# One visit per slot for the V products of an attention kernel: moved batch softmaxes, a fourth bank for the score maxima, and V products in one of the scores' PSUM banks

## The chip, the core and the metric

The kernel runs on one core of a Trainium2 chip. The metric is the device time of one execution in microseconds (us). Before the change the median of three runs is 297.95 us (297.89 to 298.03). The profile is one further execution; its span, from the first to the last instruction, is 299.0 us. Engines are named as in the profile: PE (TensorE, matmuls), PEld (its weight loads), DVE (VectorE), ACT (ScalarE), POOL (GpSimd), SP (SyncE).

## What is computed

An attention over 8 batches, 12 heads, 448 tokens and a head size of 64, followed by a soft mixture of experts with 32 slots (8 experts of 4 slots). Cut to what matters:

```python
scores = matmul(q, k.transpose(0, 1, 3, 2)) / sqrt(64)
m = max(scores, axis=-1)
e = exp(scores - m)
x = (e / (sum(e) + exp(-m) + 1e-9)) @ v        # -> x: 3584 tokens x 768
logits = x @ phi                                # 3584 x 32
d = softmax(logits, axis=0); slot_in = d.T @ x  # over all tokens
slot_out[e] = relu(slot_in[e] @ w1[e]) @ w2[e]  # 768 -> 1024 -> 768
out = softmax(logits, axis=1) @ slot_out
```

## The kernel before

Heads are taken in pairs: 48 pairs, six to a batch. The order of the work on every engine is written out by hand. A short list of words (`ramp`, lines 716 to 757) orders the first pairs; a loop over **slots** `s` (lines 758 to 832), one per pair from 3 on, orders the rest; then follow the last softmax and the expert layers (from line 843). The loop is what the change rewrites.

What a slot holds, with the functions' names:

- **A** (L285 and L304 on PE, L287 and L307 on DVE): the maxima. PE computes the scores of a later pair once into a bank of pool `psA`, and DVE reduces that bank to one maximum per row. Seven such tiles belong to a pair: two heads for each of three blocks of 128 tokens, and one tile for the last 64 tokens of both heads.
- **Bk** (L367, L370, L396, L399 on PE, L372 and L402 on ACT): PE computes the same scores transposed into a bank of pool `psB`, a second matmul (the bias, with `sel` and `mT`) subtracts the maximum, and ACT takes the exponential out of the bank. A pair has four blocks `i`; i = 0, 1, 2 fill two banks each and i = 3 fills one: seven exponentials. In the loop the matmuls of A and Bk alternate between the two halves of the PE rows, so two run side by side.
- **T** (L256 on PE): 28 small transposes of q and k for a pair six slots ahead, into one `psB` bank; a copy empties it, on ACT (L263) where n % 6 is 1 or 3, on DVE (L265) otherwise.
- **AV** (L436 on PE): the products of the exponentials with V, 32 matmuls per pair, into the one bank of pool `psV`. **N1** (L449, ACT) copies that bank to `ubuf`; **N2** (L464, L465 on DVE; L469, L479, L480 on POOL) divides.
- **PX** (L501 on PE, L507 on ACT): the turn of x, four matmuls into one `psB` bank and a copy, for the pair two slots back.
- **W1** (POOL), **W2** (L336, L337 on PE), **W3** (L342, L345, L348 on ACT): once per three pairs the maxima are turned into the bias `mT`, and into `ec`, the exponentials of the negative maxima.
- **P(b)**: the softmaxes and the slot sums of a finished batch, six parts at places `at_z`: `l_mm` (L535, 24 matmuls), `l_ev` (L558, ACT) and `c_max`; `l_turn`; `s_max`; `exps` and `corr` (L596, L601 on ACT); `c_turn`; `s_mm` (L623, 28 matmuls) with `s_add` (L632, DVE).

The order of one slot before, two half visits: blocks 0 and 1, then the second half of the V products of pair s-1 and N1; then blocks 2 and 3, T, W2 and W3, the first half of the V products of pair s, PX. PSUM has eight banks: three in `psA`, four in `psB`, one in `psV`. A pool hands out the bank that was given back first in the program's order. A slot uses nine or ten `psB` banks in turn (2, 2, 2, 1 for the blocks, T, PX, and the bias where there is one), so a matmul that needs a bank waits for ACT or DVE to empty the tile about four places back.

```python
psA = pool("psA", 3, space=PSUM)
psB = pool("psB", 4, space=PSUM)
psV = pool("psV", 1, space=PSUM)
```

The work of a slot repeats every six slots, since T's copy goes by n % 6, W2 and W3 by s % 3 and P(b) by the batch. "Slot type" below is s modulo 6. Before, types 1 and 3 have T's copy on ACT; types 2 and 5 have the bias; `l_mm` falls in type 2, `exps` in type 4 and `s_mm` in type 0.

Of the kernel before, what the change touches and what calls it, by code (L numbers as in the profile page):

```python
# [31 lines left out]
def kernel(  # L32
# [21 lines left out]
    NPAIR = B * PB  # L54
# [102 lines left out]
    with ExitStack() as at:  # L157
# [4 lines left out]
        psB = pool("psB", 4, space=PSUM)  # L162
        psV = pool("psV", 1, space=PSUM)
        pb_ = lambda nm: psB.tile([128, 512], F32, tag="b", name=nm)
        nat = {}
        ubuf = pu.tile([128, 2, 7 * W65], F32, name="ubuf")

# [73 lines left out]
        def T(n):  # L241
            g, pl = divmod(n, NP)
            first = n < NP * NP
            ps = psB.tile([128, 2, S], BF16, tag="b", name="ps_t")

            k0 = [psB.tile([128, 2, S], BF16, tag="b", name="ps_k") for _ in range(2)] if n == 0 else None
            for a in range(2):
                src = nat["qk"[a], g]
                order = [(tok, hl) for tok in range(7) for hl in range(2)]
                if a and n == 0:  # L250
                    order.sort(key=lambda z: kcol(z[1], z[0]))
                for tok, hl in order:
                    c = kcol(hl, tok) if a else (2 * tok if tok < 4 else 2 * tok - 7) * 64
                    r = slice(64 * hl, 64 * hl + 64)
                    o = k0[c // 256][r, 0, c:c + 64] if a and n == 0 else ps[r, a, c:c + 64]
                    nc.tensor.transpose(o, src[r, pl, tok * D:(tok + 1) * D], ident[r, r])  # L256
            t = qk_t[n % NQK]
            if n == 0:
                nc.scalar.copy(t[:, 0, :], ps[:, 0, :])
                nc.vector.tensor_copy(t[:, 1, 0:256], k0[0][:, 0, 0:256])  # L260
                nc.vector.tensor_copy(t[:, 1, 256:S], k0[1][:, 0, 256:S])
            elif first or n % 6 in (1, 3):
                nc.scalar.copy(t, ps)  # L263
            else:
                nc.vector.tensor_copy(t, ps)  # L265
            qkT[n] = t
# [7 lines left out]
        def A(n, i, steps=False):  # L274
            g, pl = group[n]
            if g not in mx:
                mx[g] = psm.tile([128, 21], F32, tag="mx", name="mx")
            t = qkT[n]
            if steps:
                m = mx[g]  # L280

                def run(hl):
                    r = slice(64 * hl, 64 * hl + 64)
                    ps = psA.tile([128, 512], F32, tag="a", name="ps_a")
                    nc.tensor.matmul(ps[:, 0:S], t[r, 0, i * 128:(i + 1) * 128], t[r, 1, :], start=True, stop=True)  # L285
                    c = HG * i + 2 * pl + hl
                    nc.vector.reduce_max(m[:, c:c + 1], ps[:, 0:S], axis=AX.X)  # L287

                return [lambda: run(0), lambda: run(1)]
            if i < 3:  # L290
                pss = [psA.tile([128, 512], F32, tag="a", name="ps_a") for _ in range(2)]
                for hl in range(2):
                    r = slice(64 * hl, 64 * hl + 64)
                    nc.tensor.matmul(pss[hl][:, 0:S], t[r, 0, i * 128:(i + 1) * 128], t[r, 1, :],  # L294
                                     start=True, stop=True)
                for hl in range(2):
                    c = HG * i + 2 * pl + hl
                    nc.vector.reduce_max(mx[g][:, c:c + 1], pss[hl][:, 0:S], axis=AX.X)  # L298
            else:
                ps = psA.tile([128, 512], F32, tag="a", name="ps_a")  # L300

                for hl in range(2):
                    r = slice(64 * hl, 64 * hl + 64)
                    nc.tensor.matmul(ps[64 - 64 * hl:128 - 64 * hl, 0:S], t[r, 0, 384:448], t[r, 1, :],  # L304
                                     start=True, stop=True)
                c = 3 * HG + pl
                nc.vector.reduce_max(mx[g][:, c:c + 1], ps[:, 0:S], axis=AX.X)  # L307
# [32 lines left out]
        def W3(g):  # L340
            t = psm.tile([128, S], BF16, tag="mT", name="mT")
            nc.scalar.copy(t, st["ps_m"][:, 0:S])  # L342
            mT[g] = t
            e = psm.tile([128, NP, 7], F32, tag="ec", name="ec", bufs=3)
            nc.scalar.activation(e[:, :, 0:6].rearrange("p l (i h) -> p i l h", i=3),  # L345
                                 ngm[g][:, 0:18].rearrange("p (i l h) -> p i l h", i=3, h=2),
                                 AF.Exp, scale=scale)
            nc.scalar.activation(e[:, :, 6], ngm[g][:, 18:21], AF.Exp, scale=scale)  # L348
            ec[g] = e
# [65 lines left out]
        def av_tile(n):  # L415

            if n >= NPAIR - 3:
                return psA.tile([128, 512], F32, tag="a", name="ps_av")
            return psV.tile([128, 512], F32, tag="v", name="ps_av")

        def AV(n, i, qs):
            g, pl = divmod(n, NP)
# [93 lines left out]
        def P(b):  # L516
# [1 line left out]
            eng = nc.gpsimd if b < B - 2 else nc.vector  # L518
            x = xb[b % 2]
            v = {}  # L520
            pa = lambda shape, dt, nm: psA.tile(shape, dt, tag="a", name=nm)
            flat = lambda t: t.rearrange("p i s -> p (i s)")

            def l_mm(js):
# [138 lines left out]
        post = {}  # L663
        for b in range(B - 1):
            for z, f in enumerate(P(b)):
                at_z = (0, 1, 2, 4, 5, 9) if late(b) else (0, 1, 2, 3, 4, 6)
                post.setdefault(2 * (PB * b + PB + 2) + at_z[z], []).append(f)

        ub = ubuf.rearrange("p n c -> p (n c)").bitcast(BF16)
# [32 lines left out]
        def slot_loads(s):  # L702
# [6 lines left out]
            if s % 3 == 0 and g - 2 < NG - 1:  # L709
# [3 lines left out]

        ramp = ("T0 A A T1 A A W0 T2 A G0 A X0 J0 A B0.0 A B0.1 A A T3 A B0.2 A A T4 C0.3 V0.0 W1 A V0.1 V0.2 A X1 T5 "
                "A B1.0 A K0 V0.3 H0 C1.1 N0 B1.2 A T6 C1.3 V1.0 V1.1 A B2.0 M0 K1 A T7 B2.1 A V1.2 V1.3 W2 T8 H1 A "
                "N1 B2.2 Y2 V2.0 X2 C2.3 Z0 V2.1 M1 K2 ")
        for word in ramp.split():
            op, arg = word[0], [int(z) for z in word[1:].split(".") if z]  # L720
            if op == "T":
# [7 lines left out]
            elif op == "X":  # L729
                W2(*arg)  # L730
                W3(*arg)
            elif op == "V":
                AV(*arg, range(3))
            elif op == "H":
# [20 lines left out]
                PX(0)  # L755
            elif op == "K":
                slot_loads(*arg)
        for s in range(3, NPAIR + 1):
            for y in range(2):
                hs = 2 * s + y  # L760
                mix = len(runs) > 1 and runs[0][1] == 1 - y
# [12 lines left out]
                else:  # L774
                    As(1)
                if y == 0:
                    for i in (2, 3):
                        AV(s - 1, i, range(3))
                else:
                    if s < NPAIR - 6:  # L780
                        T(s + 6)
                    if s and s + 1 in firsts:
                        W2(mg(s + 1))
                        W3(mg(s + 1))
                    if s < NPAIR:
                        for i in (0, 1):
                            AV(s, i, range(3))
# [2 lines left out]
                if y and 0 <= s - 2 < NPAIR - 2:  # L790
                    PX(s - 2)
                if y == 0:
                    if 0 <= s - 1:
                        for i in range(4):
                            AV(s - 1, i, [3])
                        if s == NPAIR:
                            PX(s - 2)
                        N1(s - 1)
                        if not on_pool(s - 1):
                            N2(s - 1)  # L800
                else:
                    if 0 <= s - 1 and on_pool(s - 1):
                        N2(s - 1)
                if y == 0 and s and s + 1 in firsts:
                    W1(mg(s + 1))
                if y == 0 and wait_loads:
                    f, z = wait_loads.pop()
                    f(z)
                if y == 0 and s % 3 == 2 and (s + 1) // 3 < NG:
                    if s == NPAIR - 4:  # L810
                        V(NG - 1)
                    if s - 1 in half_at:
                        load_half(half_at[s - 1], 0, w_tile(half_at[s - 1]))
                if y == 0 and s - 1 in stage_at:
                    stage_rows(*stage_at[s - 1][0])
                if y == 0 and s - 2 in half_at:
                    load_half(half_at[s - 2], 1)
                if y == 0 and s - 2 in stage_at:
                    stage_rows(*stage_at[s - 2][1])
                if y == 0 and hs in rows_at:  # L820
                    load_rows(rows, rows_at[hs])
                    rows = rows_at[hs]
            if s > 2 and s + 2 in firsts:
                wait_loads.append((slot_loads, s))
            else:
                slot_loads(s)
            if 2 * s + 1 in rows_at:

                if 2 * s + 1 == 89:
                    load_rows(7, 9)  # L830
                load_rows(rows + 2 * (rows == 7), rows_at[2 * s + 1])
                rows = rows_at[2 * s + 1]
        load_rows(rows, 35)
        nc.gpsimd.memset(spread, 0.0)
        for i in range(4):
            r = slice(NS * i, NS * i + NS)
# [195 lines left out]
```

## Time and profile before

| what | value |
| --- | --- |
| median of three runs | 297.95 us |
| the profiled execution: span, first to last instruction | 299.0 us |
| PE, DVE, ACT, POOL busy | 271.4, 249.7, 249.8, 195.9 us |
| granted clock of PE, slots' loop | 1.00 |
| six stretches of six slots each, from first exponential to first exponential (slots 3 to 38) | 28.18, 28.92, 29.62, 30.78, 29.49, 29.64 us |
| T's copy: ACT (L263), DVE (L265), mean of one | 928, 615 ns |

The only time on record for the profiled execution is its span. Busy time counts an instruction from its start to its end; instructions of one engine overlap there by some tens to hundreds of ns, so the start-to-start distance of instructions that follow each other is the better price of one. The six stretches run from 33.95 us to 210.58 us, from the first exponential of a slot s with s % 6 = 3 to the next such; they cover slots 3 to 38.

### The profile page before, as it was taken

What the parts mean: (1) busy time and instruction counts of PE and PEld (TensorE: products, weight loads), DVE (VectorE), ACT (ScalarE), POOL (GpSimd) and SP (SyncE); (2) the same over time, 40 slices, a digit from 0 to 9 for tenths busy, and PEclk for the clock granted to TensorE, in tenths of its full rate; (3) what the DMA queues carried; (4) which work ended last, traced back from release to release, by engine and by line L of the source; (5) the groups of instructions that cost most, each with busy time, mean ns of one, the idle gap of its engine ahead of it and who ended that gap; (6) DMA issues with size and microseconds to landing.
All of it is one profiled execution on the core that took longest, in us unless ns stands there. A gap on an engine that the chain in (4) does not pass through costs nothing.

```text
span 299.0 us, 12398 instructions
## 1 busy us (share of the span) xinstructions
PE 271.4 (91%) x5174; PEld 162.5 (54%) x5174; DVE 249.7 (84%) x581; ACT 249.8 (84%) x559; POOL 195.9 (66%) x391
## 2 busy tenths in 40 slices
PE   5999899999999999999899999999999999996820
PEld 4445456566666566566556666656665555652100
DVE  5899799999999989999889999998999675537930
ACT  3569999999899989998989899989999987337820
POOL 8792887979696979887879697978686633000000
PEclk9999999999999999999999999999999999997555
DMA  7999998999999999999999999999799989908997
GB/s 132 147 143 208 149 138 138 188 165 188 185 204 179 184 176 202 163 182 182 202 159 184 176 199 152 196 183 196 125 150 187 213 185 263 344 10 318 380 453 322
DMA packets 47015, 58.67 MB, mean 196 GB/s; under 512 B 2800, under 2 KB 39920, under 8 KB 46704
## 3 DMA queue, kind: packets, MB, share of 16 engines
q0 software_dynamic: 40304, 42.29, 89.6%
q1 hardware_dynamic: 6656, 15.60, 13.8%
q8 instruction: 40, 0.66, 0.8%
q14 instruction: 15, 0.12, 0.1%
HBM read 89.16 MB, written 15.14 MB: 349 GB/s over the span
## 4 chain that ended last, share of the span: by engine, by line
PE 68%; ACT 10%; DVE 6%; POOL 6%; issue 4%; DMA 2%; DVEq 0%; POOLq 0%; ACTq 0%
PE ps_av L436 15%; PE ps_a L285 10%; PE ps_b L367 7%; PE ps_b L370 7%; PE ps_t L256 5%; PE ps_b L396 5%; PE ps_x L501 3%; PE ps_b L399 3%; ACT W L402 2%; PE ps_o L925 2%; DVE mx L298 2%; PE ps_s L623 2%; PE ps_h L862 2%; PE ps_so L882 2%; ACT W L263 2%
## 5 line engine op out<-in xcount | busy, mean ns | idle before, releaser
L287 DVE TENSOR_REDUCE mx<-ps_a 128x1 f32<-128x448 f32 x250 | 137.3, 613 | 4.6 <-PE ps_a L285 3.5
L372 ACT ACTIVATE W<-ps_b 128x448 bf16<-128x448 f32 x250 | 120.4, 574 | 0.0
L285 PE MATMUL ps_a<-W 64*128 64x448 bf16 x250 | 80.9, 352 | 0.0
L367 PE MATMUL ps_b<-W 64*128 64x448 bf16 x250 | 70.5, 352 | 1.1
L436 PE MATMUL ps_av<-W 128*128 128x65 bf16 (+1 forms) x1536 | 64.9, 196 | 2.2 <-issue 1.6
L436 PEld LDWEIGHTS <-W 128*128 128x128 bf16 (+1 forms) x1536 | 50.5, 100 | 30.2 <-issue 26.4
L370 PE MATMUL ps_b<-mT,sel 64*128 64x448 bf16 x250 | 66.5, 350 | 0.0
L469 POOL TENSOR_TENSOR W<-ubuf,rec 128x384 bf16<-128x384 f32 x44 | 36.3, 824 | 35.7 <-ACT W L507 19.3
L402 ACT ACTIVATE W<-ps_b 128x448 bf16<-128x448 f32 x86 | 46.1, 574 | 2.0 <-PE ps_b L399 2.0
L256 PEld LDWEIGHTS <-W 64*64 64x64 bf16 x1344 | 29.3, 112 | 12.7 <-issue 4.3
L507 ACT CAST W<-ps_x 128x512 bf16<-128x512 f32 x47 | 28.6, 608 | 7.4 <-PE ps_x L501 7.2
L256 PE MATMUL ps_t<-ident,W 64*64 64x64 bf16 x1330 | 30.6, 195 | 2.4 <-ACT W L215 1.4
L307 DVE TENSOR_REDUCE mx<-ps_a 128x1 f32<-128x448 f32 x48 | 29.5, 615 | 1.4 <-PE ps_a L304 1.4
L285 PEld LDWEIGHTS <-W 64*128 64x128 bf16 x250 | 23.4, 94 | 9.8
L114 POOL DMA_DIRECT2D W<-in_moe_w_dram x30 | 22.6, 755 | 7.9 <-PE ps_b L399 7.8
L370 PEld LDWEIGHTS <-sel 64*128 64x128 bf16 x250 | 19.6, 94 | 14.4 <-issue 5.6
L396 PE MATMUL ps_b<-W 64*64 64x448 bf16 (+1 forms) x134 | 27.1, 374 | 0.3
L449 ACT COPY ubuf<-ps_av 128x455 f32<-128x455 f32 x44 | 25.1, 571 | 0.8 <-POOL W L408 0.6
L399 PE MATMUL ps_b<-mT,sel 64*64 64x448 bf16 (+1 forms) x134 | 25.1, 354 | 0.1
L263 ACT COPY W<-ps_t 128x896 bf16<-128x896 bf16 x21 | 19.5, 927 | 6.5 <-PE ps_t L256 6.5
L298 DVE TENSOR_REDUCE mx<-ps_a 128x1 f32<-128x448 f32 x38 | 21.1, 616 | 1.9 <-PE ps_a L294 1.9
L480 POOL TENSOR_TENSOR W<-ubuf,rec 128x128 bf16<-128x128 f32 x44 | 17.5, 398 | 3.7
(156 smaller groups left out, 446.6 us busy)
## 6 DMA issues: line engine op xcount, KB each, us to landing
W<-in_moe_w_dram POOLq DMA_DIRECT2D x24, 768.0 KB, 9.9
W<-in_v_dram POOLq DMA_DIRECT2D x32, 192.0 KB, 6.5
out_dram<-W SPq DMA_DIRECT2D x2, 2688.0 KB, 10.0
W<-in_q_dram POOLq DMA_DIRECT2D x15, 336.0 KB, 6.3
W<-in_k_dram POOLq DMA_DIRECT2D x15, 336.0 KB, 7.5
stage<-in_moe_w_dram POOLq DMA_DIRECT2D x4, 768.0 KB, 9.6
W<-stage SPq DMA_DIRECT2D x4, 576.0 KB, 7.3
out_dram<-W SPq DMA_DIRECT2D x6, 384.0 KB, 3.0
```

Source lines behind the costliest of these rows:

```text
L256: nc.tensor.transpose(o, src[r, pl, tok * D:(tok + 1) * D], ident[r, r])
L285: nc.tensor.matmul(ps[:, 0:S], t[r, 0, i * 128:(i + 1) * 128], t[r, 1, :], start=True, stop=True)
L287: nc.vector.reduce_max(m[:, c:c + 1], ps[:, 0:S], axis=AX.X)
L307: nc.vector.reduce_max(mx[g][:, c:c + 1], ps[:, 0:S], axis=AX.X)
L367: nc.tensor.matmul(pss[hl][:, 0:S], t[rs[hl], 1, cols], t[rs[hl], 0, :], start=True, stop=False)
L370: nc.tensor.matmul(pss[hl][:, 0:S], sel[rs[hl], 2 * pl + hl:2 * pl + hl + 1].to_broadcast([64, 128]), mT[mg(n)][rs[hl], :], start=False, s ...
L372: nc.scalar.activation(e[:, hl, :], pss[hl][:, 0:S], AF.Exp, scale=scale)
L396: nc.tensor.matmul(outs[hl], t[rs[hl], 1, cols], t[rs[hl], 0, :], start=True, stop=False)
L399: nc.tensor.matmul(outs[hl], sel[rs[hl], 2 * pl + hl:2 * pl + hl + 1].to_broadcast([64, m]), mT[mg(n)][rs[hl], :], start=False, stop=True)
L402: nc.scalar.activation(e, p[:, 0:S], AF.Exp, scale=scale)
L436: nc.tensor.matmul(o, eT[n, i, hl][:, qc], vp[g % 2][:, 2 * pl + hl, i, 0:W65], start=(i == 0 and u == 0 and hl == 0) or (u == 3 and i == ...
L469: eng.tensor_mul(x[:, 0:3, c:c + 128].rearrange("p i (h d) -> p i h d", h=2), u[:, 0:6, 0:D].rearrange("p (i h) d -> p i h d", h=2), rec[: ...
```

## The change

The steady loop now runs over slots 3 to 44 in a new order, and the old loop is kept for the last slots alone. Per slot: blocks 0, 1, 2, 3; T; N2 of the pair before; parts of P(b); then all V products of pair s with PX between them; W2 and W3's copy of `mT`; the products of the last 64 rows; N1; and W4, the two exponentials that were the second part of W3. `pa_` takes the single `psV` bank into the turn of the `psA` banks, four in all, and the V products take a `psB` bank instead. T's copy moves from DVE to ACT for n % 6 = 4. The parts of P(b) move: `exps` from slot type 4 to 5; the others keep their slot, but `l_mm` and `s_mm` stand between T and the V products. The ramp is reordered to match: it now ends with all of pair 2's V products.

```diff
+        turn_at = {"a": 0, "whole": True}
+        def pa_(shape, dt, nm):
+            z = turn_at["a"] = (turn_at["a"] + 1) % 4
+            if z == 0 and turn_at["whole"]:
+                return psV.tile(shape, dt, tag="v", name=nm)
+            if not turn_at["whole"]:
+                turn_at["a"] = 0
+            return psA.tile(shape, dt, tag="a", name=nm)
...
-            elif first or n % 6 in (1, 3):
+            elif first or n % 6 in (1, 3, 4):
                 nc.scalar.copy(t, ps)
...
-                    ps = psA.tile([128, 512], F32, tag="a", name="ps_a")
+                    ps = pa_([128, 512], F32, "ps_a")
...
             mT[g] = t
+
+        def W4(g):
             e = psm.tile([128, NP, 7], F32, tag="ec", name="ec", bufs=3)
...
-            return psV.tile([128, 512], F32, tag="v", name="ps_av")
+            return pb_("ps_av")
...
-                at_z = (0, 1, 2, 4, 5, 9) if late(b) else (0, 1, 2, 3, 4, 6)
+                at_z = (1, 3, 5, 6, 7, 9) if late(b) else (0, 1, 2, 3, 4, 6)
...
-        ramp = ("T0 A A T1 A A W0 T2 A G0 A X0 J0 A B0.0 A B0.1 A A T3 A B0.2 A A T4 C0.3 V0.0 W1 A V0.1 V0.2 A X1 T5 "
-                "A B1.0 A K0 V0.3 H0 C1.1 N0 B1.2 A T6 C1.3 V1.0 V1.1 A B2.0 M0 K1 A T7 B2.1 A V1.2 V1.3 W2 T8 H1 A "
-                "N1 B2.2 Y2 V2.0 X2 C2.3 Z0 V2.1 M1 K2 ")
+        ramp = ("T0 A A T1 A A W0 T2 A G0 A X0 J0 A B0.0 A B0.1 A A T3 A B0.2 A A T4 C0.3 V0.0 W1 A V0.1 V0.2 A X1 V0.3 H0 "
+                "N0 T5 A B1.0 A K0 C1.1 B1.2 A T6 C1.3 V1.0 V1.1 A M0 V1.2 V1.3 H1 N1 B2.0 K1 A T7 B2.1 A A W2 T8 B2.2 "
+                "Y2 X2 C2.3 Z0 V2.0 V2.1 M1 V2.2 V2.3 H2 N2 K2 ")
...
+        SN = NPAIR - 3
...
+        for s in range(3, SN):
+            Bk(s, 0, mix=True)
+            Bk(s, 1, mix=True)
+            if s + 1 in firsts:
+                W1(mg(s + 1))
+            half_loads(s, 0)
+            for f in post.get(2 * s, ()):
+                f()
+            Bk(s, 2, mix=True)
+            Bk(s, 3, 1)
+            if s < NPAIR - 6:
+                T(s + 6)
+            N2(s - 1)
+            for f in post.get(2 * s + 1, ()):
+                f()
+            for i in range(4):
+                if i == 2:
+                    PX(s - 2)
+                AV(s, i, range(3))
+            if s + 1 in firsts:
+                W2(mg(s + 1))
+                W3(mg(s + 1))
+            for i in range(4):
+                AV(s, i, [3])
+            N1(s)
+            if s + 1 in firsts:
+                W4(mg(s + 1))
+            if not on_pool(s):
+                N2(s)
+            half_loads(s, 1)
+            end_loads(s)
+        turn_at["whole"] = False
+        for s in range(SN, NPAIR + 1):
```

`half_loads` and `end_loads` issue the loads of weights, q, k and v that the old loop issued at the end of its half slots, in the same slots and the same order.

## Prediction

> **What bounds the kernel now.** I read the page first: its busy times, and its chain of waits, which is 68% PE and 10% ACT.
>
> ```profile
> PE 271.4 (91%) x5174; PEld 162.5 (54%) x5174; DVE 249.7 (84%) x581; ACT 249.8 (84%) x559; POOL 195.9 (66%) x391
> ```
>
> Three engines are close, so no single share decides. Next I cut the loop into stretches of six slots, one full turn of its pattern, each from a first exponential (L372) to the next; three of the six:
>
> ```profile
> 62.13:91.05 28.92, 28.73 (x595) 18.22 (x592) 27.54 (x64) 27.97 (x65) 23.84 (x46) 1.00 1.15 185
> 120.67:151.45 30.78, 29.04 (x595) 18.34 (x592) 27.89 (x65) 28.15 (x66) 24.54 (x47) 1.00 1.15 183
> 180.94:210.58 29.64, 28.97 (x595) 18.34 (x592) 27.80 (x65) 28.13 (x67) 24.37 (x47) 1.00 1.17 185
> ```
>
> The first is the undisturbed turn, 28.92 us. The other four after it are 0.70, 1.86, 0.57 and 0.72 longer, 3.85 in all; the waits name a late bias (M, 0.59 behind POOL's W1) and gaps with nothing waited for:
>
> ```profile
> 104.06 0.34 PE L336 MATMUL ps_m<-ident,W 128*128 128x128 bf16 x3 [0.59 <-POOL W L314]
> 150.01 0.37 PE L436 MATMUL ps_av<-W 128*128 128x65 bf16 x7 [1.10 <-issue]
> ```
>
> ACT first. Its timeline in a slot with nearly every kind of work (start, duration):
>
> ```profile
> 117.26 0.27 ACT L558 COPY lb<-ps_l 128x128 f32<-128x128 f32 x1
> 117.56 0.54 ACT L449 COPY ubuf<-ps_av 128x455 f32<-128x455 f32 x1
> 118.06 0.98 ACT L372 ACTIVATE W<-ps_b 128x448 bf16<-128x448 f32 x2
> 118.93 0.55 ACT L402 ACTIVATE W<-ps_b 128x448 bf16<-128x448 f32 x1
> 119.43 0.53 ACT L342 CAST mT<-ps_m 128x448 bf16<-128x448 f32 x1
> 119.86 0.23 ACT L345 ACTIVATE ec<-ngm 128x18 f32<-128x18 bf16 x1
> 119.97 0.20 ACT L348 ACTIVATE ec<-ngm 128x3 f32<-128x3 bf16 x1
> 120.16 0.59 ACT L507 CAST W<-ps_x 128x512 bf16<-128x512 f32 x1
> ```
>
> Starts lie closer than durations, so the price of one is start to start: exponential 0.42 (0.87 for two here, 0.85 at 136.71), seven in 2.99; the copy to ubuf 0.43; mT 0.43; ec 0.11 + 0.19; l_ev 0.30. The turn's cast (L507) is 0.48 (114.93 to 115.41), T's copy (L263) 0.80 (143.68 to 144.48), exps with corr 0.43 (127.12 to 127.55). Six slots of ACT: 6 x (2.99 + 0.43 + 0.48) + 2 x 0.73 for the biases + 2 x 0.80 + 0.73 for a batch = 27.2. Of 28.92 it waits 1.7. **There is little for a faster PE to win.** Where ACT waits longest, PE's timeline is this (slot type 0):
>
> ```profile
> 135.00 0.35 PE L285 MATMUL ps_a<-W 64*128 64x448 bf16 x1
> 135.27 0.79 PE L436 MATMUL ps_av<-W 128*128 128x65 bf16 x20
> 135.99 0.36 PE L285 MATMUL ps_a<-W 64*128 64x448 bf16 x1
> ...
> 137.06 0.60 PE L256 MATMUL ps_t<-ident,W 64*64 64x64 bf16 x28
> 137.60 0.54 PE L436 MATMUL ps_av<-W 128*128 128x65 bf16 x12
> 137.97 0.75 PE L623 MATMUL ps_s<-cd,W 128*128 128x32 bf16 x24
> 138.58 0.25 PE L623 MATMUL ps_s<-cd,ones 128*128 128x32 bf16 x4
> 138.68 0.38 PE L501 MATMUL ps_x<-ident,W 128*128 128x128 bf16 x4
> ...
> 138.99 0.36 PE L285 MATMUL ps_a<-W 64*128 64x448 bf16 x1
> ```
>
> PE is packed, and ACT's cast waits 0.92 for it. A 448-column matmul takes a place of 0.19 (the next pair starts 0.19 later), so from 135.00 to 135.27 some 0.09 is the change of tile shape, and so again before 135.99. A slot has five such changes.
>
> **The change part by part.** *Tile shapes.* One visit for the V products takes away two changes a slot, 2 x 0.09. That pays only where PE is what is late.
>
> *T's copy for n % 6 = 4.* ACT gets 0.80 per six slots, DVE loses 0.53 (its start-to-start). ACT's own work becomes 28.0, 0.9 under today's turn. This is on the path: in slot types 1, 3 and now 4 ACT does 2.99 + 0.80 + 0.48 + 0.43 = 4.70 without a break.
>
> *Banks.* With the V products in psB a slot takes ten or eleven of four banks. In the changed program's order each tile of blocks 2 and 3, T, the V products and PX wait for the exponential four tiles back. Work it by hand with a slot's first exponential at 0. Exponentials start at 0, 0.44, 0.87, 1.29, 1.72, 2.14, 2.57; ACT is free at 2.99. A bank is given back 0.60 after a start (duration 0.55, then 0.05: L402 ends at 129.48, the matmul that takes its bank starts at 129.53). So block 2's second score starts at 1.03, block 3 at 1.50, T at 1.90 (the fourth exponential), the V products at 2.43 (fifth), PX at 2.80 (sixth), the products of block 3 at 3.21 (seventh), the end at 3.64. **PE, ahead until then, is made to wait about 0.6 inside the blocks, where today the other half of the V products lies; then it has 1.7 us of work that gives ACT no exponential.** After the end: 0.10 to the next block, 0.19 to its bias, 0.39 from the bias to its exponential (129.54 to 129.93): 4.32 at the earliest, whatever ACT has.
>
> Slot types then, from first exponential to first exponential:
> - 1, 3, 4: ACT's 4.70; PE's end at 3.64 is hidden.
> - 0: s_mm's 0.70 now lies between T and the V products. PX starts at 3.50, its cast can start 0.42 later at 3.92 (ACT free since 2.99), the V products end at 4.32, next exponential 5.00. DVE has 7 x 0.535 + 0.53 + 0.28 + 0.39 = 4.95, no later.
> - 5: exps (0.43) move in between the fourth and fifth exponential. PX waits for the sixth, its cast starts at 3.63, mT 4.23, ubuf 4.66, ec, next exponential 5.39.
> - 2: l_mm's 0.59 between T and the V products, l_ev 0.30 on ACT. Cast 3.81, mT 4.37, ubuf 4.80, ec, 5.53.
>
> Sum: 3 x 4.70 + 5.00 + 5.39 + 5.53 = 30.02 against 28.92, **+1.10 per six slots**. Type by type, today's undisturbed slots in brackets: 0 5.00 (5.01), 1 4.70 (4.75), 2 5.53 (5.28), 3 4.70 (4.74), 4 4.70 (4.52), 5 5.39 (4.64). Nearly all of it is T's copy in type 4, exps in type 5 and the wait for PE in 2 and 5. The first stretch, mostly without batches, gives 4.70 + 4.70 + 4.97 + 4.57 + 4.70 + 5.53 = 29.17 against 28.18, +1.0. Seven turns: 1.0 + 6 x 1.10 = +7.6.
>
> *The 3.85 of disturbances.* The bias is now asked for about 1 us later after W1 could start, so I let its 0.70 go. The gaps should come again, since PE issues as many instructions; PE has slack in three slots of six, so I keep half of 3.15. Together -2.3; bounds 0 and -3.85.
>
> *Fourth bank for the maxima.* Each second block's last maximum waits for DVE today, about 0.1; with 28.0 of ACT it lies beside ACT's work: 0. *Ramp and tail.* The ramp takes a copy to ubuf more ahead of slot 3 (+0.43), the tail starts with a half visit less (20 products, 0.72, and a change or two): -0.4, bounds -1.5 and +1. POOL and loads: same instructions, hidden by POOL's fifth of idle time; 0.
>
> Sum: 7.6 - 2.3 - 0.4 = +4.9 on the span of 299.0, 303.9. The median lies 1.05 under the span: **302.8 us**. An error of 0.1 per slot is 4.2 us: 298 to 308.
>
> **Rivals.** *PE is the bound (faster).* For it: PE has 68% of the chain and stands packed in types 0 and 2. Then every slot keeps its two changes: 42 x 2 x 0.09 = 7.6, about 290; ACT's 28.0 allows it. It decides if PE's waits for banks stay under 0.2 a slot and ACT keeps a queue through the V products. Half-way, with ACT waiting half of today's 1.7 and the disturbances halved, it is 28.85 a turn: 295. Against it: the 4.32 loop above, and that exponentials alone feed ACT. The Trainium skill (TensorEngine Tiling (Array Packing), Key Properties) says that a change of tiling mode drains TensorE; the trace agrees with 0.09 a change, and by that rule alone the time would be this rival's 290. *Nothing (same)*: the +1.10 is met by the disturbances and an ACT idle 0.5 less per turn, 298. *Worse*: POOL's W1 comes later than M in types 2 and 5, 14 slots x 0.4 on top: 308.
>
> **Chances.** Forecast 0.66, worse 0.05, same 0.06, faster 0.23. A measurement here tells 0.2% from no change. So slower 0.71, same 0.06, faster 0.23. The range takes half-way faster (295, a little under) and the ledger's upper end: 294 to 308.
>
> **What would show it.** After: ACT's sum per turn up by 0.8; T's copy on ACT three times in six; turns of about 30.0; waits of the cast L507 (new line 520) behind PX in types 0, 2 and 5 with some 2 us a turn; PE starting block 2's second score just behind an exponential's end. Wrong if turns are under 28.9, if these casts do not wait, or if type 4 stays at 4.5.

## The result, and the profile after

| | before | after |
| --- | --- | --- |
| median (lowest to highest) of 4 runs, us | 297.99 (297.89 to 298.12) | 307.48 (306.39 to 309.17) |
| ratio to before, 95% interval | | 1.031 (1.026 to 1.035) |
| profiled execution: span, us | 299.0 | 306.7 |
| its own time, us | not on record | 308.49 |

The kernel is 9.5 us slower; forecast was 4.9. In the runs after the change, and in those of the next section, the time is 1.7 to 1.9 above the span. The profiled execution of before, span 299.0, therefore took about 300.8 (an estimate from the 1.8 of those runs, not measured), 2.85 above its median. For the comparison I use a second profile of the kernel before, run as a control: span 296.8, time 298.54. Against it the spans differ by 9.9.

The busy times, and the chain of waits, of after:

```profile
PE 274.5 (90%) x5174; PEld 169.0 (55%) x5174; DVE 247.4 (81%) x574; ACT 255.1 (83%) x566; POOL 196.1 (64%) x391
...
ACT 42%; PE 40%; issue 6%; DMA 3%; POOL 3%; DVE 2%; DVEq 0%; ACTq 0%; POOLq 0%
```

The chain was 68% PE and 10% ACT; now ACT has 42% of it and PE 40%. The chain passes back and forth between the two, as it would in a loop between them.

Three stretches of six slots of after (from, to, length; busy time of PE, PEld, DVE, ACT, POOL; clock; then the DMA share and GB/s):

```profile
65.18:95.28 30.10, 29.28 (x595) 19.13 (x593) 27.08 (x63) 28.73 (x68) 23.75 (x47) 1.00 1.12 182
...
156.79:186.99 30.20, 29.40 (x595) 19.17 (x593) 27.31 (x64) 28.83 (x68) 24.18 (x47) 1.00 1.11 177
186.99:217.20 30.21, 29.35 (x595) 19.14 (x593) 27.28 (x64) 28.84 (x69) 24.30 (x48) 1.00 1.14 182
```

and two of the control:

```profile
62.20:91.11 28.91, 28.68 (x595) 18.24 (x592) 27.61 (x64) 27.96 (x65) 23.82 (x46) 1.00 1.14 185
...
178.85:207.83 28.98, 28.80 (x595) 18.26 (x592) 27.73 (x65) 28.02 (x67) 24.33 (x47) 1.00 1.17 187
```

The full clock is granted in all of them. An undisturbed turn is 30.20 after (forecast 30.02) and 28.95 before. ACT's busy time rises by 0.8 a turn: T's copy. The rest of the 1.25 is time in which ACT has nothing to do.

The difference of the spans, by place: up to the first exponential of slot 3 +1.8 (35.81 against 34.03); slots 3 to 38 +7.6 (181.39 against 173.80); slots 39 to 43 +1.3 (23.82 against 22.51); what follows -0.8 (65.65 against 66.42). Sum 9.9.

Why a turn is longer shows in one slot. ACT of after in slot type 2:

```profile
181.38 2.85 ACT L385 ACTIVATE W<-ps_b 128x448 bf16<-128x448 f32 x6
183.93 0.74 ACT L415 ACTIVATE W<-ps_b 128x448 bf16<-128x448 f32 x1
184.77 0.27 ACT L571 COPY lb<-ps_l 128x128 f32<-128x128 f32 x1
185.37 0.58 ACT L520 CAST W<-ps_x 128x512 bf16<-128x512 f32 x1 [0.33 <-PE ps_x L514]
185.92 0.53 ACT L353 CAST mT<-ps_m 128x448 bf16<-128x448 f32 x1
186.35 0.55 ACT L462 COPY ubuf<-ps_av 128x455 f32<-128x455 f32 x1
...
186.99 0.55 ACT L385 ACTIVATE W<-ps_b 128x448 bf16<-128x448 f32 x1
```

Seven exponentials run back to back for 3 us. Then ACT is idle for 0.10 ahead of the logits' copy and for 0.33 ahead of the cast, which waits for the turn of x. Cast, mT, ubuf and the next exponential start 3.99, 4.54, 4.97 and 5.61 behind the first one; worked out were 3.81, 4.37, 4.80 and 5.53. And PE of after in type 0, whose first exponential starts at 171.65:

```profile
172.25 0.78 PE L380 MATMUL ps_b<-W 64*128 64x448 bf16 x2
...
173.57 0.61 PE L267 MATMUL ps_t<-ident,W 64*64 64x64 bf16 x28
174.11 0.77 PE L636 MATMUL ps_s<-cd,W 128*128 128x32 bf16 x24
...
175.18 0.39 PE L514 MATMUL ps_x<-ident,W 128*128 128x128 bf16 x4
175.40 0.78 PE L449 MATMUL ps_av<-W 128*128 128x65 bf16 x20
176.11 0.36 PE L296 MATMUL ps_a<-W 64*128 64x448 bf16 x1
```

Two scores that follow each other at once take 0.53 to 0.55 together; block 2's take 0.78, so the second starts about 0.25 late, at 172.65 or so. That is where the second exponential ends and gives a bank back (1.03 behind the first was worked out, 1.00 it is). The profile names no release at these matmuls, so this reading rests on the times, and on the experiment with one bank more (d2 below). T starts at +1.92, as worked out (1.90). From 173.57 to 176.11 PE is packed, but with nothing that feeds ACT an exponential.

### The profile page after: what moved, and what is told of

Its sections match the earlier page's. It is cut to its first block, busy times and chain, and to the rows that moved or that the text cites. A ratio compares the mean times of both kernels' runs of the same rounds, so it can differ in the third digit from the quotient of the medians.

```text
span 306.7 us, 12382 instructions
## 1 busy us (share of the span) xinstructions
PE 274.5 (90%) x5174; PEld 169.0 (55%) x5174; DVE 247.4 (81%) x574; ACT 255.1 (83%) x566; POOL 196.1 (64%) x391
## 4 chain that ended last, share of the span: by engine, by line
ACT 42%; PE 40%; issue 6%; DMA 3%; POOL 3%; DVE 2%; DVEq 0%; ACTq 0%; POOLq 0%
ACT W L385 17%; PE ps_av L449 9%; ACT ubuf L462 7%; ACT W L520 5%; ACT W L415 5%; PE ps_b L380 4%; ACT W L274 4%; PE ps_b L409 3%; PE ps_t L267 3%; DMA W<-in_k_dram 3%; PE ps_x L514 3%; PE ps_b L383 2%; PE ps_b L412 2%; PE ps_s L636 2%; PE ps_o L975 2%
## 5 line engine op out<-in xcount | busy, mean ns | idle before, releaser
L380 PE MATMUL ps_b<-W 64*128 64x448 bf16 x250 | 76.2, 353 | 5.4
L296 PE MATMUL ps_a<-W 64*128 64x448 bf16 x250 | 70.5, 353 | 0.0
L383 PE MATMUL ps_b<-mT,sel 64*128 64x448 bf16 x250 | 63.3, 355 | 0.0
L449 PEld LDWEIGHTS <-W 128*128 128x128 bf16 (+1 forms) x1536 | 54.3, 101 | 9.1 <-issue 5.1
L520 ACT CAST W<-ps_x 128x512 bf16<-128x512 f32 x47 | 30.6, 650 | 7.8 <-PE ps_x L514 7.2
L267 PEld LDWEIGHTS <-W 64*64 64x64 bf16 x1344 | 30.1, 112 | 11.8 <-issue 2.9
L274 ACT COPY W<-ps_t 128x896 bf16<-128x896 bf16 x28 | 27.9, 997 | 5.2 <-PE ps_t L267 5.2
L383 PEld LDWEIGHTS <-sel 64*128 64x128 bf16 x250 | 15.2, 94 | 30.4 <-issue 25.4
L462 ACT COPY ubuf<-ps_av 128x455 f32<-128x455 f32 x44 | 26.9, 612 | 2.7 <-PE ps_av L449 2.0
L296 PEld LDWEIGHTS <-W 64*128 64x128 bf16 x250 | 22.3, 95 | 7.2 <-issue 0.4
L380 PEld LDWEIGHTS <-W 64*128 64x128 bf16 x250 | 19.2, 94 | 11.9 <-issue 5.9
```

Of the source, the lines that this page charges most:

```text
L380: nc.tensor.matmul(pss[hl][:, 0:S], t[rs[hl], 1, cols], t[rs[hl], 0, :], start=True, stop=False)
L383: nc.tensor.matmul(pss[hl][:, 0:S], sel[rs[hl], 2 * pl + hl:2 * pl + hl + 1].to_broadcast([64, 128]), mT[mg(n)][rs[hl], :], start=False, s ...
L449: nc.tensor.matmul(o, eT[n, i, hl][:, qc], vp[g % 2][:, 2 * pl + hl, i, 0:W65], start=(i == 0 and u == 0 and hl == 0) or (u == 3 and i == ...
L462: (nc.scalar.copy if on_pool(n) else nc.vector.tensor_copy)(u, src)
L520: nc.scalar.copy(xT(b, pb), pss[0])
```

## The experiments

The kernels ran in three groups, each group beside the kernel before on one chip. "Turn" is the undisturbed turn in the profile of that kernel, the types are its six slots, from first exponential to first exponential.

| kernel | ratio (95%) | types 0 to 5 | turn |
| --- | --- | --- | --- |
| before | 1 | 5.01, 4.79, 5.26, 4.74, 4.52, 4.64 | 28.95 |
| after | 1.031 (1.026 to 1.035) | 5.05, 4.67, 5.62, 4.65, 4.67, 5.54 | 30.20 |
| c0_before_again | 0.999 (0.996 to 1.001) | as before | 28.97 |
| e1_tcopy_back | 1.029 (1.025 to 1.034) | 5.06, 4.68, 5.61, 4.66, 4.54, 5.65 | 30.20 |
| e2_tcopy_alone | 1.014 (1.007 to 1.022) | types 4 and 5: 5.10, 4.67 | 29.60 |
| e3_post_early | 1.025 (1.021 to 1.030) | types 0 and 2: 4.85, 5.49 | 29.88 |
| e4_ramp_busy | 1.035 (1.031 to 1.039) | as after | 30.21 |
| c1_one_visit_old_banks | 1.040 (1.035 to 1.045) | 5.18, 4.73, 5.86, 4.66, 4.75, 5.44 | 30.63 |
| c2_new_banks_two_visits | 1.056 (1.051 to 1.061) | 5.40, 5.12, 5.70, 5.18, 4.87, 5.15 | 31.4 |
| c3_five_banks | 1.040 (1.034 to 1.045) | as c1 | 30.63 |
| d1_dve_light | 1.021 (1.017 to 1.024) | 5.06, 4.68, 5.61, 4.66, 4.54, 5.29 | 29.83 |
| d2_dve_light_five_banks | 1.010 (1.006 to 1.016) | 4.74, 4.67, 5.19, 4.65, 4.48, 5.28 | 29.01 |
| d3_places_back | 1.015 (1.012 to 1.018) | 4.86, 4.67, 5.65, 4.65, 4.88, 4.89 | 29.60 |
| v1_split_s_mm | 0.9984 (0.9963 to 1.0005) | types 0 and 1: 4.71, 4.98 | 28.86 |

My theory: the single visit ties PE to ACT by the scores' banks, ACT then starves behind the blocks, and T's copy and exps add to the slots where ACT is full. The rivals to it: the copy alone; where the parts of the batches stand; DVE; and the ramp.

### T's copy: back on DVE, and alone on ACT

**e1_tcopy_back**, after with

```diff
-            elif first or n % 6 in (1, 3, 4):
+            elif first or n % 6 in (1, 3):
```

> The changed kernel, but T's copy for n % 6 = 4 goes back from ACT to DVE. Theory (ACT's own work sets slots 1, 3 and 4; once the copy is gone, type 4 falls back on the loop from the seventh exponential through the last V products to the next block's first exponential, 4.33): type 4 falls from 4.67 to about 4.35, the other types stay, 7 slots x 0.32 = 2.2 us less than the changed kernel's 306.4 to 307.5: about 305. Rival (the whole 0.80 of the copy is on the path): 5.6 us less, 301 to 302. Rival (DVE is late): no gain.

307.1 us (306.08 to 308.29). Type 4 falls by 0.13 only and type 5 rises by 0.11: no gain. ACT of this kernel in type 4 (first exponential at 191.43) and type 5 (at 195.97):

```profile
194.87 0.59 ACT L520 CAST W<-ps_x 128x512 bf16<-128x512 f32 x1 [0.16 <-PE ps_x L514]
...
198.07 0.42 ACT L609 ACTIVATE cd<-z 128x256 bf16<-128x256 f32 x1 [0.25 <-POOL z L604]
```

With the copy gone, ACT waits in type 4 for PE's turn of x. In type 5 exps (L609) waits for z, which POOL computes (L604), and starts 2.10 behind the first exponential. It is late in after already, where the profile names no wait, because the exponential ahead still counts as running. POOL and ACT in type 5 of after, first exponential at 196.31:

```profile
197.73 0.53 POOL L604 TENSOR_TENSOR z<-lb,lb 128x160 f32<-128x160 f32 x1
...
198.28 0.44 ACT L609 ACTIVATE cd<-z 128x256 bf16<-128x256 f32 x1
```

There z ends 1.95 behind the first exponential and exps starts at 1.97. In e2 (next), where z is done well before, exps starts at 1.70.

**e2_tcopy_alone**, before with the opposite edit.

> The kernel before, with one line of the change alone: T's copy for n % 6 = 4 on ACT. Theory (ACT is the bound of the loop before): type 4, 4.52 with 0.2 of slack on ACT, goes to about 5.1; 7 slots x 0.6 = +4.3 us, 302.3. Rival (PE is the bound and ACT has slack): below +0.7 us.

302.21 us (301.15 to 305.09), as expected. ACT of this kernel in type 4 (start, duration):

```profile
188.85 0.66 ACT L402 ACTIVATE W<-ps_b 128x448 bf16<-128x448 f32 x1
189.27 1.03 ACT L263 COPY W<-ps_t 128x896 bf16<-128x896 bf16 x1
190.06 0.74 ACT L507 CAST W<-ps_x 128x512 bf16<-128x512 f32 x1
```

The cast starts 0.79 behind the copy and waits for nothing. In the kernel before, ACT is what is late in this slot: 0.58 of the copy's 0.80 reach the end of the slot.

### Where the parts of the batches stand

**e3_post_early**, after with `l_mm` and `s_mm` half a slot earlier, ahead of blocks 2 and 3:

```diff
-                at_z = (1, 3, 5, 6, 7, 9) if late(b) else (0, 1, 2, 3, 4, 6)
+                at_z = (0, 3, 5, 6, 7, 8) if late(b) else (0, 1, 2, 3, 4, 6)
```

> The changed kernel, but l_mm and s_mm of the late batches stand before block 2 instead of between T and the V products (at_z 0 and 8 instead of 1 and 9). Theory (PE waits about 0.6 before block 2 for banks of exponentials, and PE work behind T delays the V products and with them the next exponential): type 0 from 5.05 to about 4.65, type 2 from 5.62 to about 5.25, 0.75 a turn, 6 turns: 4.5 us less than the changed kernel, about 302. Rival (the moved work costs the same anywhere, or the two more changes of tile shape per part cost what the V products' visit saved): 0 to +2 us.

306.09 us (304.73 to 307.2). The sign is right, the size less than half: type 0 gains 0.20, type 2 0.13. The wait was in part only moved: in type 0 the fifth exponential now waits 0.15 for its score, which stands behind `s_mm`, and the cast still waits 0.34 for the turn of x, which stands behind the banks.

**d3_places_back**, after with the copy on DVE and every part of P(b) in the slot type in which before had it (`l_mm` and `s_mm` ahead of block 2, as in e3):

```diff
-            elif first or n % 6 in (1, 3, 4):
+            elif first or n % 6 in (1, 3):
...
-                at_z = (1, 3, 5, 6, 7, 9) if late(b) else (0, 1, 2, 3, 4, 6)
+                at_z = (0, 1, 3, 4, 5, 8) if late(b) else (0, 1, 2, 3, 4, 6)
```

> The changed kernel with T's copy for n % 6 = 4 back on DVE and the batch parts at other places: exps back in type 4, l_mm and s_mm before block 2 (at_z 0, 1, 3, 4, 5, 8). The single visit and the banks stay. Theory (about half of the loss is where the batch parts and the copy were put, the rest the visit itself): type 5 from 5.54 to about 5.1, type 4 about 4.75, type 0 4.85, type 2 5.49, a turn near 29.5: 302 to 303. Rival (the visit alone makes the loss): 306 to 307.

303.5 us (302.32 to 304.21), close to the 302 to 303 expected. Type 5 falls to 4.89 and type 4 rises to 4.88: exps is back in type 4. Of the change's 3.1% about half, some 4 us, is the new places with the copy; the other half (1.5%) stays with the single visit, its banks and its ramp.

### The banks and the visits, one by one

**c0_before_again** is the kernel before once more.

> The kernel before once more, unchanged, for its profile. The first profile of it showed 3.85 us of late biases and gaps over six turns. If these belong to most executions, its turns again average about 29.7 and the median lies under the span as there; if they were that execution's own, turns near 28.95 and a span of about 296.

298.22 us (297.41 to 299.59, ten runs). It shows what a profile of an ordinary execution looks like: turns of 28.17, 28.91, 29.61, 29.16, 28.97 and 28.98, where the first profile had up to 30.78.

**c1_one_visit_old_banks**, after with the banks of before:

```diff
-        turn_at = {"a": 0, "whole": True}
+        turn_at = {"a": 0, "whole": False}
...
-            return pb_("ps_av")
+            return psV.tile([128, 512], F32, tag="v", name="ps_av")
```

> The changed kernel with the banks of before: the maxima in three banks, the V products in a bank of their own, the scores with four to themselves. Theory (the single visit is what costs, and a fourth bank for the maxima is what it needs): not faster than the changed kernel; the fourth-last maxima of a slot hold the block of the last 64 rows back by 0.2 to 0.8 where DVE lags, 307 to 313. Rival (the loss comes from the V products sitting in one of the scores' banks): back to about the kernel before, 298 to 300.

310.72 us (309.92 to 311.65). PE of this kernel in type 2:

```profile
183.40 0.35 PE L296 MATMUL ps_a<-W 64*128 64x448 bf16 x1 [0.18 <-DVE mx L298]
```

With three banks for the maxima, PE waits for DVE in block 2, and the new scores behind that matmul wait with it.

**c2_new_banks_two_visits**, before with the new banks (`pa_` as in the change), the order untouched.

> The kernel before with the change's banks alone: maxima in four banks, V products in one of the four score banks, two visits per slot and T's copy and the batch parts as before. Theory (the visit costs, not the banks): the fourth score of a slot now waits for the first exponential, 0.1 a slot or less: 298 to 302. Rival (the banks cost): most of the loss, 304 to 308.

315.6 us (315.0 to 316.21), far above what I had expected. PE of this kernel:

```profile
202.03 0.35 PE L378 MATMUL ps_b<-W 64*128 64x448 bf16 x1 [0.19 <-ACT W L383]
...
202.52 0.79 PE L447 MATMUL ps_av<-W 128*128 128x65 bf16 x20
```

In two visits the V products hold one of the scores' four banks from the first half (end of a slot) to the copy behind the second half, in the middle of the next (here the second half starts at 202.52, its copy at 203.39). Blocks 0 and 1 make do with three banks, and the score waits for an exponential; between 36 and 216 us it does so 29 times, 5.7 us in all. Slots 3 to 38 are 14.5 longer than in the control; what makes up the rest is open. The four kernels of two orders by two sets of banks (before; the new order with the old banks; the old order with the new banks; both, from the first comparison) give 298.2, 310.7, 315.6 and 307.5. So the new banks alone cost 17 us, the new order alone 12, and both together 9.5: each takes away part of what the other costs. The new order here is the single visit together with the new places and T's copy; no run has the single visit with the old banks and nothing else.

**c3_five_banks**, after with three banks for the maxima and five for scores and V products together:

```diff
-        psB = pool("psB", 4, space=PSUM)
-        psV = pool("psV", 1, space=PSUM)
+        psB = psV = pool("psB", 5, space=PSUM)
...
-        turn_at = {"a": 0, "whole": True}
+        turn_at = {"a": 0, "whole": False}
```

> The changed kernel with five banks shared by scores, T, turn of x, bias and V products, and three for the maxima. Theory (PE waits before block 2 for banks of exponentials, and what lies behind T then comes late): T starts at the third exponential's end, 1.47 instead of 1.90, and types 0 and 2 lose 0.4 each against the kernel with the banks of before and one visit, some 5 us less than that one. Rival (the wait is for the last exponential itself, which no bank shortens, or for DVE): the same as that one within 1.5 us.

310.36 us (310.28 to 311.37), the same slots as c1. My theory's gain did not come; the rival did, which named the last exponential or DVE. To tell the two apart, DVE had to be taken out of the way.

### DVE out of the way

**d1_dve_light** is e1 with cheaper maxima: in the loop DVE reduces 224 of the 448 columns and leaves out the rest. **d2_dve_light_five_banks** is c3 with the same and T's copy on DVE:

```diff
-                    nc.vector.reduce_max(m[:, c:c + 1], ps[:, 0:S], axis=AX.X)
+                    nc.vector.reduce_max(m[:, c:c + 1], ps[:, 0:S // 2], axis=AX.X)
...
-                nc.vector.reduce_max(mx[g][:, c:c + 1], ps[:, 0:S], axis=AX.X)
+                nc.vector.reduce_max(mx[g][:, c:c + 1], ps[:, 0:S // 2 if n > 5 else S], axis=AX.X)
```

> The changed kernel with T's copy for n % 6 = 4 back on DVE (as in e1), and each maximum taken over 224 of the 448 columns in the loop: DVE's main work is cut by almost half, everything else stays (the maximum only shifts both sides of the softmax). Theory (in e1 type 4 stopped at 4.54 because DVE was late; the other types wait for ACT and PE): type 4 falls to about 4.35 and type 5 back to 5.5, the others stay within 0.05; a turn of 29.8 to 29.9 against 30.2, some 2 us less than e1, 305. Rival (DVE holds the whole merged visit back): every type falls towards ACT's own work, a turn near 28, 293.

> The same as d1, but with five banks shared by scores, T, turn of x, bias and V products, and three for the maxima, which DVE now empties in time. Theory (PE's waits for banks of exponentials put T, s_mm and l_mm late): T starts about 0.4 earlier; type 0 falls from 5.05 to about 4.6, type 2 from 5.6 to about 5.15, the others by 0.1 at most; 5 us less than d1. Rival (the V products wait for the last exponential, which no bank shortens): the same as d1 within 1.5 us.

d1: 305.06 us (304.18 to 306.15). Type 5 falls from e1's 5.65 to 5.29, also below after's 5.54. With less work on DVE, POOL's z ends 1.29 behind the first exponential (2.07 in e1, 1.95 in after), and exps starts at 1.71 (2.10 and 1.97). In after and e1 POOL had waited 1.27 for DVE (L585) ahead of type 4; in d1 it does not. So DVE was late, by way of POOL, with T's copy and without it. Type 4 stays at 4.54, with the same wait of 0.16 for the turn of x: DVE wasn't its bound, which was my reading of e1 until then, and that part fell. d2: 301.02 us (300.44 to 303.95), 4.0 less than d1 (5 expected). PE in type 2 of d1, whose first exponential starts at 179.73:

```profile
180.45 0.78 PE L380 MATMUL ps_b<-W 64*128 64x448 bf16 x2
...
181.77 0.61 PE L267 MATMUL ps_t<-ident,W 64*64 64x64 bf16 x28
```

and of d2, where it starts at 175.30:

```profile
175.65 0.72 PE L379 MATMUL ps_b<-W 64*128 64x448 bf16 x2
...
176.91 0.61 PE L266 MATMUL ps_t<-ident,W 64*64 64x64 bf16 x28
```

One more bank lets block 2 start at +0.35 instead of +0.72, and T at +1.61 instead of +2.04. The 0.43 of T is the 0.42 by which the slot gets shorter (5.61 to 5.19); type 0 gains 0.32, and the full slots 1 and 3 nothing. In the window from 36 to 216 us the cast waits for the turn of x 6 times and 2.7 us, where in d1 it does 16 times and 6.8 us. This is the theory's main step, shown by one edit, with DVE's work cut; with all of it (c3) the gain doesn't appear. Even so the turn is 29.01 and the kernel 1.0% slower than before: its profile is 1.9 longer than the control's, and 1.3 of that is the ramp (first exponential of slot 3 at 35.33 against 34.03).

### The ramp

**e4_ramp_busy**, after with 44 idle matmuls on PE ahead of the bias of slot 3, whose results are overwritten:

```diff
+            if g == 2:
+                for _ in range(44):
+                    nc.tensor.matmul(ps[:, 0:64], ident, ident[:, 0:64], start=True, stop=True)
```

> The changed kernel, with 44 idle matmuls of 64 columns in the ramp ahead of the bias of slot 3, where PE waits 1.56 us and the profile then shows 3.4 us at half clock (33.3 to 36.7 us). Theory (the wait lowers the granted clock, which costs the ramp about 1.5 us in some executions and makes the changed kernel's times spread over 2.8 us): the clock stays at 1.00 there, the profiled ramp is about 1.5 us shorter, times near the fastest of the changed kernel, 306.4, with less spread. Rival (the clock falls for another reason, such as time since the start): the same fall and the same spread.

308.56 us (308.2 to 309.97). The clock stays at 1.00 there and the first exponential of slot 3 comes at 34.64 instead of 35.81, yet the time is not less. The last matmul of the outputs is 1.5 earlier (290.68 against 292.21), and the program ends 16.1 behind it where after needs 14.5. Why the end took longer is open. The profiles of e3, c1, c3, d1, d2 and d3 have no half clock between 16 us and slot 3 either, without the idle matmuls; e1's has one earlier, from 15.9 to 22.7. So e4 doesn't show that the wait is the cause.

### A version of before

In the kernel before, ACT waits longest for PE in type 0, where the slot sums stand. **v1_split_s_mm** is before with the slot sums in two parts, 16 matmuls in type 0 and 12 in type 1:

```diff
-            def s_mm():
+            def s_mm(j0=0, j1=KC + 1):
...
-                at_z = (0, 1, 2, 4, 5, 9) if late(b) else (0, 1, 2, 3, 4, 6)
+                at_z = (0, 1, 2, 4, 5, 9, 10) if late(b) else (0, 1, 2, 3, 4, 6)
```

> The kernel before, two visits and all, with the slot sums of the late batches (s_mm, 28 matmuls, and s_add) split over two slots: 16 matmuls in type 0, where PE and DVE are both full (5.01), and 12 in type 1, where ACT sets 4.76 and PE has room. Theory: type 0 falls by about 0.3, type 1 rises by 0.05 at most, 6 turns: 1.5 us less than before, 296.5. Rival (PE has no room in type 1 either, or one more change of tile shape and one more add eat it): 298 to 298.5.

298.29 us (297.28 to 300.48, twelve runs). Type 0 gains 0.30, type 1 gives 0.19 back. The turn is 0.1 shorter, and the time can't be told from no change. No version here beats the kernel before.

## Why the prediction was right or wrong, point by point

- **Direction and mechanism: right.** "There is little for a faster PE to win" fits: e2 puts 0.65 on the turn with one more copy on ACT, and v1, which takes work from PE where it is late, wins 0.1. PE ran into the scores' banks inside the blocks, and d2 against d1 shows the price.
- **Tile shapes: no gain from them shows**, as said. The Trainium skill (TensorEngine Tiling (Array Packing), Key Properties) has a change of tiling mode drain TensorE; two changes a slot fewer left the turn 1.25 longer, so the rule is no guide to the time where PE isn't what is late.
- **The slot ledger: right in the sum, 0.18 a turn low.** Worked out 30.02, measured 30.20; types 0, 1, 3 and 4 within 0.05, type 2 0.09 low and type 5 0.15 low. In type 5 a wait was left out: exps starts 1.97 behind the first exponential, 0.02 behind the end of POOL's z, where 1.71 is its place without a wait (d1, and type 5 is 5.29 there). So the prediction's 0 for POOL is about 0.25 a turn too low, and without that wait its 5.39 is 0.10 too high. `c_turn` (L640) was left out too; it stands on PE between T and the V products, 0.28 from 199.04 to the first V product at 199.32, but d1 has it there as well. Both come with parts that moved: not only `exps` changes its slot type, as the text ahead of the prediction has it, but by `at_z` `l_turn`, `s_max` and `c_turn` as well, each to the next type. The step that was forecast +7.6 over the slots measures +8.9 (7.6 to slot 38, 1.3 in slots 39 to 43).
- **T's copy: half right.** Type 4 is 4.67 (4.70 worked out) with ACT full. But taking the copy away brings it only to 4.54 (e1), so something else stands close behind. It isn't DVE (d1). The traces of e1 and d1 name PE's turn of x there (0.16); that this is the loop worked out at 4.32 is argued and not shown, and one more bank (d2) takes the slot only to 4.48. In the kernel before, the same copy does reach the end of the slot (e2).
- **The fourth bank for the maxima at 0: too low.** With three, and the V products in a bank of their own, the merged visit takes 3.2 us more (c1). The ledger came out right because it counts no wait of PE for DVE's maxima, which four banks make true.
- **The disturbances, -2.3: the step that failed.** They were read off one execution whose time was about 2.85 above the median. The control's turns have 0.9 of them over its 28.95, after's have 1.1 over its 30.20 (30.86 and 30.65), so nothing was given back. The late bias did go (in after L347 doesn't wait in the third turn), but other gaps came: in that turn ACT waits 0.45 for ps_av and 0.30 for ps_m, each behind a gap on PE with nothing waited for (0.21 and 0.17). "The median lies 1.05 under the span" failed with it: a time is 1.8 above its span.
- **Ramp and tail, -0.4: wrong sign, +1.0.** The one copy more (+0.43) was seen. Not seen: with pair 2's products all behind the bias, PE has nothing to do while POOL's W1 is late, and all 32 products still to do when it comes. In the control the wait is split around V products, 0.62 and 0.55. After, PE stands still once:

```profile
32.13 0.34 PE L347 MATMUL ps_m<-ident,W 128*128 128x128 bf16 x3 [1.56 <-ACT W L415]
...
33.17 1.75 PE L449 MATMUL ps_av<-W 128*128 128x65 bf16 x32
```

The profile names the exponential that ended at 32.10; POOL's W1 (L325), whose tile L347 reads, ended at 32.08. The bias comes no later than in the control (32.13 against 32.09), but behind it the control has 6 products left. In this execution half a clock then follows (last section). It is worth about 0.9 of the 1.8: e3, with the same ramp and no half clock, has the first exponential of slot 3 at 34.93 instead of 35.81.

Put right, from the control's span: 296.8 + 7.6 + 1.3 (ledger's error) + 0 + 1.0 = 306.7, the span measured. With the disturbances at 0 and nothing else changed, the forecast would have been 298.2 + 7.2 = 305.4. The result lies 0.5 under the upper end of the range. That margin was meant for an error of 0.1 per slot; the ledger was 0.03 per slot low, and what used the margin up was the disturbances and the ramp. That the range held is in part luck. The lower rivals (290, 295, 298) didn't come; POOL's W1, the rival at 308, gives a time close to the result, but by another way: in the slots M doesn't wait for W1, only in the ramp does something of the kind happen, and what waits for POOL in a slot is exps, for z.

The signs named beforehand: ACT's sum +0.8, there; turns of about 30.0, 30.2; block 2's second score just behind an exponential's end, there; T's copy on ACT in three slots of six, there. The waits of the cast were to be 2 us a turn in types 0, 2 and 5: they are 1.1, 0.80 in type 0 and 0.33 in type 2; in type 5 no wait of the cast is named; there it is exps that comes late, behind POOL's z.

**Open:** why e4's end came later; why some executions of the same kernel have the half clock in the ramp and others don't; and the spread of after itself (306.4 to 309.2), wider than that of before.

## What to carry to other kernels

Price a slot by start-to-start times on the fullest engine and follow, tile by tile, which release each matmul waits for; here that gave a turn within 0.2 of 30. Where durations overlap a wait can go unnamed: compare an instruction's start with the end of what it reads. Moving all work of one kind behind one point saves changes of tile shape, but leaves the engine that it doesn't feed without work, and a bank's worth depends on the order it stands in: judge both together. Take the base from an execution whose time is known and near the median, and don't book its disturbances as a gain.

## What the runs showed of the hardware

In one execution of after the granted clock halved behind a PE wait of 1.56 us. The wait alone isn't enough: d1 and d3 wait 1.58 and 1.57 at the same place and keep the full clock. PE of after in one of the microseconds at half clock (start and end, length, busy, clock third from the right):

```profile
34.00:35.00 1.00, 1.00 (x20) 0.81 (x20) 0.00 (x0) 0.20 (x2) 1.00 (x2) 0.50 1.26 204
```

The clock is 0.50 from about 33.3 to 36.7, while PE is busy all the time; in the 3.47 us ahead of it PE was busy 55% (1.91). The Trainium skill (TensorE: Matmul & The Clock Gate, Part 1, What's actually happening) gives a free-running window of 3413 ns, and half the rate after an idle one. The length agrees (3.4); that the window must be idle does not, since PE ran matmuls at both ends of the stretch ahead. That the phase runs free would fit that only some executions show it, which no run here settles.
